# Attention's product with v in plain fp32, two heads side by side in the array, and x written as one tensor

## The chip, the cores and the metric

The kernel runs on one core of a Trainium2 chip. The metric is the device time of one execution in microseconds (us), less is better. Five engines work side by side, each in its own instruction order: PE (TensorE, matrix products and transposes, results in PSUM), DVE (VectorE), ACT (ScalarE), POOL (GpSimd, which reads and writes SBUF alone) and SP (SyncE, which here only issues DMAs). PSUM has eight banks of 128 x 512 fp32.

## The reference

Attention over 4 batches of 8 heads with 576 tokens and 64 columns a head, then two dense layers over all 2304 tokens:

```python
q_rot, k_rot = (rotate(q), rotate(k))
scores = scale * np.matmul(q_rot, k_rot.transpose(0, 1, 3, 2))
scores = scores - np.max(scores, axis=-1, keepdims=True)
attn = np.exp(scores)
attn = attn / (np.sum(attn, axis=-1, keepdims=True) + 1e-09)
x = np.matmul(attn, v)                      # (4, 8, 576, 64), then to (2304, 512)
...
h = np.maximum(x @ w_in, 0.0);  x = h * h @ w_out          # w_in 512 x 2048, w_out 2048 x 512
h = x @ w_in2;  g = np.maximum(h, 0.0) + alpha * np.minimum(h, 0.0);  out = g @ w_out2
```

All of it is fp32 (the weights arrive as 64-bit numbers and are converted on the chip).

## The kernel before

**Products.** Where the kernel wants more than one fp32r pass carries, it splits an operand into a high part (a copy rounded to fp32r) and a low part (the value minus its high part) and adds up fp32r products of the parts. Transposes go through PE with an identity, in fp32.

**Attention.** Two heads of a batch make a pair, 16 pairs in all. A pair has nine steps (`order`): four blocks of 128 queries for each of two heads j, and one step for the last 64 queries of both heads. One loop runs over all 144 steps s. In step s it issues the scores of step s (`scores`, L208: a high and a low product with k into a PSUM tile `sc`; DVE takes the negated row maximum `nm`, L211; ACT takes the exponential into `p` with the row sums, L212) and, four steps later (LAG), the transposes of that step's P (`trans`, L229: four 128 x 128 transposes into a bank `ps`; `trans_tail`, L241 to L248, for the last 64 keys). `split` empties the bank: ACT copies the high part `pth` (L217), then DVE subtracts it from the same bank into the low part `ptl` (L218). Both read PSUM, one after the other, and only then is the bank free. There are three such banks (`ps_t`), shared with the transposes of the next pair's rotated k and q.

**The next pair's k and q.** `turn(n + 1)` runs in steps 0, 1 and 2 of pair n: transposes of k and q (L155, L161) into `ps` banks, a split into `nat` (ACT L149, then DVE L150), and in `stack` (L176) twelve DMAs on SP that lay out `kH`, `kL` and `qT` for the scores of the next pair. Scores of pair n + 1 wait for these DMAs.

**The product with v.** `vsplit` (POOL, L133 and L134) splits v of one pair and lays high and low side by side, so that a head's v has 128 columns: 64 high and 64 low. `pv(n, j, hf, st)` is one head's product for one half of the queries (288): five chunks of 128 keys, for each a product with `pth` and one with `ptl`, ten matmuls of 288 columns into one PSUM bank `acc` (the only one, NAC = 1), rows 0 to 63 from v's high and 64 to 127 from its low part. DVE (L277) or ACT (L279) copies the bank to `st`. A pair has four such bursts, in the steps OP + x * OPD after its last transposes (0, 2, 4 and 6 steps later). `xd` in device memory has two addends per head (the two row halves), written with one DMA per head (L281). `over` (L257 to L265) writes one over the row sums to `rd`.

**The dense layers.** `load_x` reads both addends (L514) and the row factors (L516), `join_x` adds the addends (L524) and multiplies (L525) on POOL, then x is split too (L533, L541). The first two blocks of 384 tokens (FIRST) and the first weights are read and converted in the last 24 steps of attention (AHEAD_X), in `follow`. From there on PE runs the layers' products (L550 to L552, L568) while DVE and ACT convert weights.

**What sets the order.** PE's and SP's order is the order of the code (manual schedule), since the loop above emits it step by step; `at_step` puts a function into a later step. On DVE, ACT and POOL a scheduler orders attention's work by its estimates; in the dense layers their order too is by the code.

Of the kernel before, what the change touches and what calls it, by code (L numbers as in the profile page):

```python
# [22 lines left out]
P = 128  # L23
KC = DM // P
# [10 lines left out]
KQB, STB, PTB = 2, 2, 3  # L35
RB = 1
ROPE_AT, TURN_AT = 5, (0, 1, 2)
AHEAD_X = 24
OP0, OPD0, OP1, OPD1 = 1, 1, 0, 1
OP, OPD, OV = 0, 2, 11  # L40


def attention(tc, q, k, v, ident_d, rope_d, xd, rd, follow):
# [10 lines left out]
    with ExitStack() as at:  # L54
# [12 lines left out]
        lds.append(scored.enter_context(tc.tile_pool(name="ald1", bufs=1)))  # L67
# [21 lines left out]
        raw = {(x, nm): lds[(x, nm) == (1, "v")].tile([P, 4, 5, D], F32, name=f"{nm}raw{x}") for x in range(2) for nm in "kqv"}  # L89
# [36 lines left out]
        vv, ops = {}, {}  # L126

        def vsplit(n):

            x = raw[n // 2 % 2, "v"][:, 2 * (n % 2):2 * (n % 2) + 2]  # L130
            t = sm.tile([P, 2, NQ, 2, D], F32R, name="vs", bufs=KQB)
            hi, lo = t[:, :, :, 0], t[:, :, :, 1]
            G.tensor_copy(out=hi, in_=x)  # L133
            G.tensor_tensor(out=lo, in0=x, in1=hi.bitcast(F32), op=ALU.subtract)  # L134
            vv[n] = t

# [78 lines left out]
        def split(dst, src, sl):  # L215
            hi, lo = dst
            A.activation(out=sl(hi), in_=src, func=AF.Copy)  # L217
            V.tensor_tensor(out=sl(lo), in0=src, in1=sl(hi).bitcast(F32), op=ALU.subtract)  # L218

        def trans(n, i, j):  # L220

            if (i, j) == (0, 0):
                PT[n, "tail"] = tuple(pt.tile([P, S], F32R, name=f"ptt{x}", bufs=2) for x in "hl")
            if i == 0:
                PT[n, j] = tuple(pt.tile([P, 4, S], F32R, name=f"pt{x}") for x in "hl")
# [5 lines left out]
            if i < 4:  # L231
                split(PT[n, j], uv, lambda t: t[:, :, i * P:(i + 1) * P])
            else:
                for x in range(2):
                    split(PT[n, x], uv[:, :, 64 * x:64 * x + 64], lambda t: t[:, :, 512:576])

        def trans_tail(n, i0, i1):
# [5 lines left out]
            if m:  # L243
                split(PT[n, "tail"], u[:, 0:m * P], lambda t: t[:, i0 * P:(i0 + m) * P])
            if i1 == 5:
# [3 lines left out]
                for x in range(2):  # L249
                    rs, u0 = slice(64 * x, 64 * x + 64), (m + x) * P + 64 * x  # L250
                    split(PT[n, "tail"], u[rs, u0:u0 + 64], lambda t: t[rs, 512:576])
# [15 lines left out]
        def pv(n, j, hf, st):  # L267
            vs = vv[n]
            sl = slice(hf * SH, (hf + 1) * SH)
            acc = ps_t.tile([P, 512], F32, name="ps", tag="t") if (n, j) == (len(pairs) - 1, 1) else ps_a.tile([P, 512], F32, name="acc")  # L270
            for c in range(NQ):
                for x in range(2):
                    t = PT[n, j][x][:, c, sl] if c < 4 else PT[n, "tail"][x][:, sl]
                    T.matmul(acc[:, 0:SH], lhsT=vs[:, j, c].rearrange("p y d -> p (y d)"), rhs=t,  # L274
                             start=(c == 0 and x == 0), stop=(c == 4 and x == 1))
            if hf == 0:
                V.tensor_copy(out=st[j][:, sl], in_=acc[:, 0:SH])  # L277
# [32 lines left out]
        at_step(0, vsplit, 0)  # L310
# [3 lines left out]
        for s in range(len(steps) + LAG + OP + 3 * OPD + 8):  # L314
            if s < len(steps):
                n, i, j = steps[s]
                at = s % per
                if at == 0 and n + 1 < len(pairs):
                    at_step(s + OV, vsplit, n + 1)
                    for x, (f, *a) in zip(TURN_AT, turn(n + 1)):  # L320
                        at_step(s + x + (1 if n == 0 else 0), f, *a)
                if at == ROPE_AT and n + 2 < len(pairs):
# [5 lines left out]
                    if n % 2 and n + 3 < len(pairs):  # L328
                        for nm in "kqv":
                            load((n + 3) // 2, nm)  # L330
                scores(n, i, j)
            if LAG <= s and s - LAG < len(steps):
# [3 lines left out]
                if (i, j) == ((2, 1) if last else (3, 1)):  # L336
                    trans_tail(n, 0, 3 if last else 4)
                    sts[n] = [sm.tile([P, S], F32, name=f"st{x}", bufs=STB) for x in range(2)]
                    for x in range(2 if last else 0):
                        at_step(s + OP0 + x * OPD0, pv, n, x, 0, sts[n])  # L340
                if (i, j) == (4, 0):
                    trans_tail(n, 3 if last else 4, 5)
                    at_step(s, over, n)
                    for x in range(4):
                        if not last:
                            at_step(s + OP + x * OPD, pv, n, x % 2, x // 2, sts[n])
                        elif x // 2:
                            at_step(s + OP1 + x % 2 * OPD1, pv, n, x % 2, 1, sts[n])
# [75 lines left out]
def moe(tc, xd, rd, mats, pbias, dram, al, out):  # L424
# [11 lines left out]
    with ExitStack() as mo:  # L436
# [7 lines left out]
        XT = pool("xt", 1, side="right").tile([P, 2, 3, W], F32, name="xt")  # L444
# [63 lines left out]
        def load_x(layer, b, c):  # L508
            c0 = b * W
            k = next(xbuf)  # L510
            xr, r = XT[:, k, 0:2], XT[:, k, 2]
            if layer == 0:
                for j in range(2):
                    nc.sync.dma_start(out=xr[64 * j:64 * j + 64],  # L514
                                      in_=xd[j, :, c, c0:c0 + W].rearrange("(y d) c -> d y c", y=2))
                    nc.sync.dma_start(out=r[64 * j:64 * j + 64], in_=rd[c, j:j + 1, c0:c0 + W].to_broadcast([D, W]))  # L516
            else:
                nc.sync.dma_start(out=xr[:, 0], in_=x2[:, c, c0:c0 + W])
            xin[layer, b, c] = xr, r

        def join_x(layer, b, c):
            xr, r = xin[layer, b, c]
            if layer == 0:
                G.tensor_tensor(out=xr[:, 0], in0=xr[:, 0], in1=xr[:, 1], op=ALU.add)  # L524
                G.tensor_tensor(out=xr[:, 0], in0=xr[:, 0], in1=r, op=ALU.mult)  # L525

        def high_x(layer, b, c):
# [4 lines left out]
            if first(layer, b):  # L532
                G.tensor_copy(out=xh, in_=xin[layer, b, c][0][:, 0])  # L533
# [214 lines left out]
```

## Time and profile before

| | us |
|---|---|
| three runs | 1148.27, 1149.08, 1150.41; median 1149.08 |
| span of the profiled execution, first to last instruction | 1145.5 |
| median less span | 3.6 |
| PE busy in the span | 1082.2 (94%) |
| DVE, ACT, POOL busy | 684.6, 573.1, 374.5 |
| one pair in the middle of attention | 18.29 |
| attention's last product with v starts | about 337 |
| first dense product starts | about 339.5 |

The page gives no time of its own for the profiled execution beyond its span, so its own time is taken as the span with the 3.6 us around it. Attention takes the first 340 us and the dense layers the other 805. A row of the chain of waits (the critical chain) gives a start, a length and the engine and line on which the program's end hung there; a row of waits gives who waited for whom, the sum, the count and the longest; a row of a stretch gives the busy time of each engine in it (instructions in brackets), the granted TensorE clock, the DMA engines' mean busy share and GB/s.

### The profile page before, as it was taken

How to read it: one execution, taken by the hardware profiler on the slowest of the kernel's cores; microseconds unless marked ns; L12 is line 12 of the kernel's file. 1: busy time of each engine (PE TensorE's matmuls, PEld its weight loads, DVE VectorE, ACT ScalarE, POOL GpSimd, SP SyncE). 2: the span in 40 equal slices, each digit the busy share in tenths (PEclk: the TensorE clock that was granted, in tenths of full speed). 3: DMA queues.
4: the chain of work that ended last, by engine and by line, in shares of the span. 5: the costliest groups of instructions: out<-in, count | busy, mean ns of one | idle time of the engine just before them, and what ended most of it. 6: DMA issues, size and time to landing. Idle time of an engine off the chain costs nothing.

```text
span 1145.5 us, 17940 instructions
## 1 busy us (share of the span) xinstructions
PE 1082.2 (94%) x6480; PEld 1031.5 (90%) x6480; DVE 684.6 (60%) x1215; ACT 573.1 (50%) x1236; POOL 374.5 (33%) x360
## 2 busy tenths in 40 slices
PE   2899999999879999999999999999999999999997
PEld 1789898988779999899999999998999989898996
DVE  3888888888678997769597751323232323323231
ACT  1787888878648864465555634223232322323231
POOL 3885558755640000132131311041321405032230
PEclk9999999999989999999999999999999999999999
DMA  6768666775774443557767558810101020010101
GB/s 150 179 181 215 181 167 164 207 199 158 192 214 138 147 129 92 180 184 229 234 207 251 181 180 255 280 51 16 40 8 50 1 50 7 21 35 14 29 1 27
DMA packets 97495, 150.18 MB, mean 131 GB/s; under 512 B 21760, under 2 KB 66432, under 8 KB 97408
## 3 DMA queue, kind: packets, MB, share of 16 engines
q1 hardware_dynamic: 91312, 137.96, 42.3%
q10 hardware_dynamic: 5840, 10.96, 2.9%
q8 instruction: 51, 0.84, 0.3%
q14 instruction: 36, 0.29, 0.1%
q0 software_dynamic: 256, 0.13, 0.0%
HBM read 84.98 MB, written 35.73 MB: 105 GB/s over the span
## 4 chain that ended last, share of the span: by engine, by line
PE 81%; DVE 6%; DMA 5%; SPq 4%; issue 1%; ACT 1%; POOL 1%; ACTq 0%; DVEq 0%; POOLq 0%
PE py L568 31%; PE ph L550 11%; PE ph L552 11%; PE ph L551 11%; PE acc L274 5%; PE sc L208 4%; PE ps L229 3%; SPq L176 3%; PE ph L568 2%; DMA kraw<-in_k_dram 2%; DVE nat L150 2%; DMA xt<-x 1%; DMA xt<-r 1%; DVE ptl L218 1%; DVE nm L211 1%
## 5 line engine op out<-in xcount | busy, mean ns | idle before, releaser
L550 PE MATMUL ph<-xs,w 128*128 128x384 f32 x768 | 256.9, 334 | 1.0 <-ACT g L590 1.0
L551 PE MATMUL ph<-xs,w 128*128 128x384 f32 x768 | 256.7, 334 | 0.0
L552 PE MATMUL ph<-xs,w 128*128 128x384 f32 x768 | 256.6, 334 | 0.0
L503 DVE TENSOR_TENSOR gl<-g,gh 128x384 fp32r<-128x384 f32 x192 | 111.0, 581 | 169.7 <-PE py L568 112.1
L594 POOL TENSOR_TENSOR g<-g,xt 128x384 f32<-128x384 f32 x96 | 101.9, 1062 | 295.5 <-DVE xt L593 295.5
L590 ACT ACTIVATE g<-ph 128x384 f32<-128x384 f32 x192 | 94.3, 491 | 201.6 <-PE ph L552 192.6
L496 ACT ACTIVATE gh<-g 128x384 fp32r<-128x384 f32 x192 | 100.3, 523 | 150.7 <-PE py L568 135.5
L568 PE MATMUL py<-w,gh 128*128 128x512 f32 x504 | 155.3, 389 | 0.0
L568 PE MATMUL py<-gh,w 128*128 128x384 f32 x560 | 145.7, 334 | 0.0
L550 PEld LDWEIGHTS ph<-xs,w 128*128 128x128 f32 x768 | 144.3, 188 | 1.5 <-ACT g L590 1.3
L551 PEld LDWEIGHTS ph<-xs,w 128*128 128x128 f32 x768 | 144.3, 188 | 0.2
L552 PEld LDWEIGHTS ph<-xs,w 128*128 128x128 f32 x768 | 144.3, 188 | 0.0
L593 DVE TENSOR_SCALAR xt<-ph,al 128x384 f32<-128x384 f32 x96 | 59.3, 618 | 138.8 <-ACT g L590 132.2
L212 ACT ACTIVATE p<-sc,nm 128x576 f32<-128x576 f32 x144 | 106.5, 741 | 23.5 <-DVE nm L211 8.6
L211 DVE TENSOR_REDUCE nm<-sc 128x1 f32<-128x576 f32 x144 | 105.7, 750 | 16.7 <-PE sc L208 15.2
L218 DVE TENSOR_TENSOR ptl<-ps,pth 128x512 fp32r<-128x512 f32 (+1 forms) x160 | 99.7, 631 | 20.7 <-ACT pth L217 18.3
L568 PEld LDWEIGHTS py<-w,gh 128*128 128x128 f32 x504 | 94.5, 188 | 19.4
L217 ACT ACTIVATE pth<-ps 128x512 fp32r<-128x512 f32 (+1 forms) x160 | 87.0, 554 | 40.9 <-PE ps L229 35.3
L568 PEld LDWEIGHTS py<-gh,w 128*128 128x128 f32 x560 | 101.5, 188 | 0.0
L568 PE MATMUL py<-w,gl 128*128 128x512 f32 x252 | 98.1, 389 | 0.0
L229 PE MATMUL ps<-ident,p 128*128 128x128 f32 x576 | 87.9, 276 | 8.2 <-DVE nat L150 7.4
L568 PE MATMUL py<-gl,w 128*128 128x384 f32 x280 | 93.6, 334 | 1.9 <-DVE gl L503 1.9
(119 smaller groups left out, 1904.2 us busy)
## 6 DMA issues: line engine op xcount, KB each, us to landing
w<-in_moe_w_in_dram SPq DMA_DIRECT2D x32, 512.0 KB
w<-in_moe_w_out_dram SPq DMA_DIRECT2D x32, 512.0 KB
wk<-xs SPq DMA_DIRECT2D x32, 512.0 KB
w<-wk SPq DMA_DIRECT2D x30, 512.0 KB
xt<-x SPq DMA_DIRECT2D x72, 192.0 KB
x<-st ACTq DMA_DIRECT2D x32, 288.0 KB
kH<-nat SPq DMA_DIRECT2D x62, 144.0 KB
qT<-nat SPq DMA_DIRECT2D x62, 144.0 KB
```

The source lines that it names most:

```text
L211: V.tensor_reduce(out=nm, in_=sc[:, :, 0:SH], axis=AX.XY, op=ALU.max, negate=True)
L212: A.activation(out=Pt[n, i][:, j * S:(j + 1) * S].rearrange("p (a b) -> p a b", a=2), in_=sc[:, :, 0:SH], func=AF.Exp, bias=nm, accum_out= ...
L218: V.tensor_tensor(out=sl(lo), in0=src, in1=sl(hi).bitcast(F32), op=ALU.subtract)
L229: T.transpose(u[:, c * P:(c + 1) * P], p[:, (S + 64) * j + c * P:(S + 64) * j + (c + 1) * P], ident)
L496: A.activation(out=hi, in_=hidden(layer, b, i), func=AF.Copy)
L503: V.tensor_tensor(out=lo, in0=hidden(layer, b, i), in1=gsp[u][0].bitcast(F32), op=ALU.subtract)
L550: T.matmul(ph[:, :W], lhsT=wh[:, cs], rhs=xh, start=(c == 0), stop=False)
L551: T.matmul(ph[:, :W], lhsT=wh[:, cs], rhs=xl, start=False, stop=False)
L552: T.matmul(ph[:, :W], lhsT=wl[:, cs], rhs=xh, start=False, stop=(c == KC - 1))
L568: T.matmul(acc, lhsT=x, rhs=y, start=(s0 and k == 0), stop=(s1 and k == 2))
L590: A.activation(out=g, in_=ph, func=AF.Relu)
L594: G.tensor_tensor(out=g, in0=g, in1=mn, op=ALU.add)
```

## The change

The P transposed leaves PSUM in one copy (`leave`), by ACT and DVE in turn, as fp32. `vsplit` and its pieces are gone: `pv` takes v as it was loaded, in fp32, with 64 columns. Both heads of a pair go into one PSUM bank: head 0 into rows 0 to 63, head 1 into rows 64 to 127, which are the two column halves of the array. A matmul per head and chunk of keys stands alone now (fp32 with fp32), head 0 and head 1 in turn. The work of a pair is cut into six pieces (`LUMPS`: for each half of the queries two chunks, two chunks, one chunk), one piece a step, beginning one step after the pair's last transposes. The last pair runs each half of the queries in one piece. `xd` holds one tensor, written once a pair, and `join_x` only multiplies. v's buffers move to another pool, v's load is issued 16 steps later than k's and q's (V_AT), and P transposed has two buffers of each name instead of three.

```diff
-KQB, STB, PTB = 2, 2, 3
+KQB, STB, PTB = 2, 2, 2
-ROPE_AT, TURN_AT = 5, (0, 1, 2)
+ROPE_AT, TURN_AT, V_AT = 5, (0, 1, 2), 21
+LUMPS = ((0, 0, 2), (0, 2, 4), (0, 4, 5), (1, 0, 2), (1, 2, 4), (1, 4, 5))
-OP, OPD, OV = 0, 2, 11
+OP, OPD = 1, 1
...
-        def split(dst, src, sl):
-            hi, lo = dst
-            A.activation(out=sl(hi), in_=src, func=AF.Copy)
-            V.tensor_tensor(out=sl(lo), in0=src, in1=sl(hi).bitcast(F32), op=ALU.subtract)
+        turns = itertools.cycle((A, V))
+
+        def leave(dst, src):
+            E = next(turns)
+            if E is A:
+                A.activation(out=dst, in_=src, func=AF.Copy)
+            else:
+                V.tensor_copy(out=dst, in_=src)
...
-        def pv(n, j, hf, st):
-            vs = vv[n]
+        accs = {}
+
+        def pv(n, hf, c0, c1):
+            b, hp = pairs[n]
+            v2 = raw[n // 2 % 2, "v"][:, 2 * (n % 2):2 * (n % 2) + 2]
             sl = slice(hf * SH, (hf + 1) * SH)
-            acc = ps_t.tile([P, 512], F32, name="ps", tag="t") if (n, j) == (len(pairs) - 1, 1) else ps_a.tile([P, 512], F32, name="acc")
-            for c in range(NQ):
-                for x in range(2):
-                    t = PT[n, j][x][:, c, sl] if c < 4 else PT[n, "tail"][x][:, sl]
-                    T.matmul(acc[:, 0:SH], lhsT=vs[:, j, c].rearrange("p y d -> p (y d)"), rhs=t,
-                             start=(c == 0 and x == 0), stop=(c == 4 and x == 1))
+            if c0 == 0:
+                accs[hf] = ps_t.tile([P, 512], F32, name="ps", tag="t") if (n, hf) == (len(pairs) - 1, 1) else ps_a.tile([P, 512], F32, name="acc")
+            acc = accs[hf]
+            for c in range(c0, c1):
+                for j in range(2):
+                    t = PT[n, j][:, c, sl] if c < 4 else PT[n, "tail"][:, sl]
+                    T.matmul(acc[64 * j:64 * j + 64, 0:SH], lhsT=v2[:, j, c], rhs=t, start=c == 0, stop=c == 4)
+            if c1 < NQ:
+                return
...
-            A.activation(out=st[j][:, sl], in_=acc[:, 0:SH], func=AF.Copy)
-            b, hp = pairs[n]
-            nc.scalar.dma_start(out=xd[j, :, hp, b * S:(b + 1) * S], in_=st[j])
+            A.activation(out=sts[n][:, sl], in_=acc[:, 0:SH], func=AF.Copy)
+            nc.scalar.dma_start(out=xd[:, hp, b * S:(b + 1) * S], in_=sts.pop(n))
...
             if layer == 0:
-                G.tensor_tensor(out=xr[:, 0], in0=xr[:, 0], in1=xr[:, 1], op=ALU.add)
-                G.tensor_tensor(out=xr[:, 0], in0=xr[:, 0], in1=r, op=ALU.mult)
+                G.tensor_tensor(out=xr, in0=xr, in1=r, op=ALU.mult)
```

PE in the middle of a pair, before: the end of one burst (head 0) and the start of the next (head 1), with two steps of scores (`sc`) and transposes (`ps<-ident,p`) between.

```order
L274 MATMUL acc_1676<-ptl_1420,vs_1341 128x288
L274 MATMUL acc_1676<-ptth_1417,vs_1341 128x288
L274 MATMUL acc_1676<-pttl_1418,vs_1341 128x288
L208 MATMUL sc_1689<-kH_1349,qT1_123 128x288 x2
L208 MATMUL sc_1689<-kL_1350,qT1_123 128x288 x2
L229 MATMUL ps_1701<-ident_77,p_1538 128x128 x4
L208 MATMUL sc_1731<-kH_1349,qT1_123 128x288 x2
L208 MATMUL sc_1731<-kL_1350,qT1_123 128x288 x2
L229 MATMUL ps_1741<-ident_77,p_1538 128x128 x4
L274 MATMUL acc_1748<-pth_1450,vs_1341 128x288
L274 MATMUL acc_1748<-ptl_1451,vs_1341 128x288
```

The same place of PE in the changed kernel: the end of the second piece, the third piece (last chunk, both heads) and the start of the fourth.

```order
L273 MATMUL acc_1486<-pt0_1241,vraw0_111 64x288
L273 MATMUL acc_1486<-pt1_1275,vraw0_111 64x288
L198 MATMUL sc_1531<-kH_1188,qT1_120 128x288 x2
L198 MATMUL sc_1531<-kL_1189,qT1_120 128x288 x2
L223 MATMUL ps_1539<-ident_77,p_1397 128x128 x4
L273 MATMUL acc_1486<-ptt_1240,vraw0_111 64x288 x2
L198 MATMUL sc_1549<-kH_1188,qT1_120 128x288 x2
L198 MATMUL sc_1549<-kL_1189,qT1_120 128x288 x2
L223 MATMUL ps_1557<-ident_77,p_1397 128x128 x4
L273 MATMUL acc_1563<-pt0_1241,vraw0_111 64x288
L273 MATMUL acc_1563<-pt1_1275,vraw0_111 64x288
```

Two heads alternate within a piece, and a piece stands in every step instead of a burst in every second one.

DVE around the next pair's k and q (`nat`), before: steps 0 to 2 of a pair.

```order
L211 TENSOR_REDUCE nm_1868<-sc_1863 128x1
L150 TENSOR_TENSOR nat_1826<-ps_1856,nat_1826 128x512
L218 TENSOR_TENSOR ptl_1700<-ps_1871,pth_1699 128x4x128
L211 TENSOR_REDUCE nm_1891<-sc_1886 128x1
L150 TENSOR_TENSOR nat_1826<-ps_1878,nat_1826 128x512
L218 TENSOR_TENSOR ptl_1740<-ps_1894,pth_1739 128x4x128
L218 TENSOR_TENSOR pttl_1698<-ps_1901,ptth_1697 128x512
L150 TENSOR_TENSOR nat_1826<-ps_1913,nat_1826 128x2x2x64
L211 TENSOR_REDUCE nm_1937<-sc_1932 128x1
```

The same place of DVE in the changed kernel.

```order
L201 TENSOR_REDUCE nm_1600<-sc_1595 128x1
L201 TENSOR_REDUCE nm_1625<-sc_1620 128x1
L140 TENSOR_TENSOR nat_1593<-ps_1613,nat_1593 128x512
L212 COPY pt0_1479<-ps_1628 128x4x128
L201 TENSOR_REDUCE nm_1647<-sc_1642 128x1
L140 TENSOR_TENSOR nat_1593<-ps_1634,nat_1593 128x512
L212 COPY ptt_1478<-ps_1656 128x512
L201 TENSOR_REDUCE nm_1686<-sc_1681 128x1
L140 TENSOR_TENSOR nat_1593<-ps_1662,nat_1593 128x2x2x64
```

Between the three `nat` rows two copies stand where three subtractions stood, and one row of `nm` comes earlier.

SP's queue at the very start, before: the last loads of k and q for the first pairs, and the first DMAs of `stack`.

```order
L99 DMA qraw_113<-in_q_dram 128x2x256
L107 DMA qraw_113<-in_q_dram 64x2x64 x2
L712 DMA al<-in_moe_alpha_dram 128x16x1
L176 DMA kH<-nat 64x576
L176 DMA qT_122<-nat 64x576
```

The same place in the changed kernel.

```order
L99 DMA qraw_110<-in_q_dram 128x2x256
L107 DMA qraw_110<-in_q_dram 64x2x64 x2
L386 DMA w_4004<-in_moe_w_in_dram 128x4x256
L386 DMA w_4006<-in_moe_w_in_dram 128x4x256
L708 DMA al<-in_moe_alpha_dram 128x16x1
L166 DMA kH<-nat 64x576
L166 DMA qT_119<-nat 64x576
```

Two loads of first-layer weights (512 KB each), which before stood among the loads of the last attention steps, stand at the program's start, ahead of the first pair's `stack`: their buffers no longer lie where attention's tiles lie.

## Rows read from the trace of the kernel before

**Rows 1.** The page: span, and busy time of each engine.

```profile
span 1145.5 us, 17940 instructions
PE 1082.2 (94%) x6480; PEld 1031.5 (90%) x6480; DVE 684.6 (60%) x1215; ACT 573.1 (50%) x1236; POOL 374.5 (33%) x360
```

**Rows 2.** Stretches: busy us of each engine, granted clock, DMA share, GB/s.

```profile
60.00:90.00 30.00, 27.51 (x219) 26.27 (x218) 26.82 (x50) 24.27 (x62) 23.63 (x20) 1.00 0.66 176
...
330.00:360.00 30.00, 24.94 (x133) 24.39 (x134) 21.89 (x44) 16.52 (x35) 4.30 (x4) 0.89 0.45 137
360.00:390.00 30.00, 30.00 (x175) 30.00 (x175) 27.74 (x52) 25.30 (x48) 0.00 (x0) 1.00 0.52 157
```

**Rows 3.** The chain of waits through one pair: start us, us, engine and line.

```profile
159.03 0.11 PE ps L247
159.14 0.11 PE ps L248
159.25 0.14 PE ps L260
159.39 1.32 PE acc L274 x10
...
161.23 0.44 PE ps L229 x4
...
168.87 0.53 PE sc L208 x4
...
177.68 0.40 PE acc L274 x3
```

**Rows 4.** Waits of PE from 42 to 282 us: sum us, times, longest us.

```profile
PE ps L161 <- DVE nat L150: 9.1, 13, 0.7
PE ps L229 <- DVE nat L150: 6.9, 13, 0.6
```

**Rows 5.** Groups by line, 60 to 280 us: busy us, mean ns of one.

```profile
L274 PE MATMUL acc<-ptl,vs 128*128 128x288 f32 x194 | 52.8, 294 | 0.0
...
L218 DVE TENSOR_TENSOR ptl<-ps,pth 128x512 fp32r<-128x512 f32 (+1 forms) x121 | 75.4, 631 | 11.4 <-ACT pth L217 9.5
...
L150 DVE TENSOR_TENSOR nat<-ps,nat 128x512 fp32r<-128x512 f32 (+1 forms) x36 | 21.5, 598 | 3.1 <-ACT nat L149 2.7 <-DMA kraw<-in_k_dram 0.3
...
L217 ACT ACTIVATE pth<-ps 128x512 fp32r<-128x512 f32 (+1 forms) x120 | 65.2, 555 | 24.2 <-PE ps L229 24.2
```

**Rows 6.** SP's queue after one turn: start us, us of the issue.

```profile
176.91 1.15 SPq L176 DMA_DIRECT2D kH<-nat  x2
...
183.41 1.23 SPq L176 DMA_DIRECT2D kL<-nat  x2
```

**Rows 7.** The chain early in attention: a `kL` DMA from issue to landing.

```profile
40.53 2.98 DMA kL<-nat
```

**Rows 8.** The start: SP's queue, and a stretch of four us.

```profile
7.50 0.59 SPq L712 DMA_DIRECT2D al<-in_moe_alpha_dram  x1
...
12.00:16.00 4.00, 1.54 (x6) 1.14 (x6) 2.17 (x6) 0.96 (x3) 1.65 (x2) 1.00 0.00 0
```

**Rows 9.** Waits of PE from 282 to 365 us.

```profile
PE ps L247 <- DVE pttl L218: 3.2, 1, 3.2
PE sc L208 <- DMA kL<-nat: 2.7, 2, 1.7
PE ps L260 <- DVE sums L258: 2.1, 1, 2.1
...
PE ps L260 <- DVE pttl L218: 0.9, 1, 0.9
PE ps L229 <- DVE ptl L218: 0.8, 1, 0.8
```

**Rows 10.** PE's instructions at the end of attention: start us, us, engine line.

```profile
337.06 0.44 PE L274 MATMUL ps<-pth,vs 128*128 128x288 f32 x1
337.31 0.44 PE L274 MATMUL ps<-ptl,vs 128*128 128x288 f32 x1
...
339.46 0.52 PE L550 MATMUL ph<-xs,w 128*128 128x384 f32 x1
```

More of the change, by code (lines that the diff above doesn't have):

```diff
@@ L86, in attention @@
         rot = {}
-        raw = {(x, nm): lds[(x, nm) == (1, "v")].tile([P, 4, 5, D], F32, name=f"{nm}raw{x}") for x in range(2) for nm in "kqv"}
+        raw = {(x, nm): (st_ if nm == "v" else lds[0]).tile([P, 4, 5, D], F32, name=f"{nm}raw{x}") for x in range(2) for nm in "kqv"}
         for x in range(2):
@@ L124, in rope @@
             E.tensor_tensor(out=r, in0=t1, in1=t2, op=ALU.add)
[L126 to L135, printed above, removed]
+        ops = {}
         qTs = [kq.tile([P, 2 * S + 64], F32R, name=f"qT{x}", bufs=1) for x in range(2)]
@@ L243, in trans_tail @@
             if m:
-                split(PT[n, "tail"], u[:, 0:m * P], lambda t: t[:, i0 * P:(i0 + m) * P])
+                leave(PT[n, "tail"][:, i0 * P:(i0 + m) * P], u[:, 0:m * P])
             if i1 == 5:
@@ L250, in trans_tail @@
                     rs, u0 = slice(64 * x, 64 * x + 64), (m + x) * P + 64 * x
-                    split(PT[n, "tail"], u[rs, u0:u0 + 64], lambda t: t[rs, 512:576])
+                    leave(PT[n, "tail"][rs, 512:576], u[rs, u0:u0 + 64])
         def over(n):
@@ L308, in at_step @@
             later.setdefault(s, []).append((f, a))
-        at_step(0, vsplit, 0)
         rope(1, "k")
         rope(1, "q", E=V)
-        for s in range(len(steps) + LAG + OP + 3 * OPD + 8):
+        for s in range(len(steps) + LAG + OP + len(LUMPS) * OPD + 8):
             if s < len(steps):
@@ L328, in attention @@
                     if n % 2 and n + 3 < len(pairs):
-                        for nm in "kqv":
+                        for nm in "kq":
                             load((n + 3) // 2, nm)
+                        at_step(s - ROPE_AT + V_AT, load, (n + 3) // 2, "v")
                 scores(n, i, j)
@@ L337, in attention @@
                     trans_tail(n, 0, 3 if last else 4)
-                    sts[n] = [sm.tile([P, S], F32, name=f"st{x}", bufs=STB) for x in range(2)]
-                    for x in range(2 if last else 0):
-                        at_step(s + OP0 + x * OPD0, pv, n, x, 0, sts[n])
+                    if last:
+                        at_step(s + OP0, pv, n, 0, 0, 5)
                 if (i, j) == (4, 0):
@@ L442, in moe @@
         Xw = [Xf[:, 1024 * k:1024 * k + 1024].rearrange("p (y n) -> p y n", y=2) for k in range(6)]
-        XT = pool("xt", 1, side="right").tile([P, 2, 3, W], F32, name="xt")
+        XT = pool("xt", 1, side="right").tile([P, 2, 2, W], F32, name="xt")
         st = [pool("st0", 1, side="right")]
@@ L701, in fused_kernel @@
     nc.gpsimd.memset(pbias, -float(896 * 2 ** 23))
-    xd = dram.tile([2, P, KC, NT], F32, name="x1")
+    xd = dram.tile([P, KC, NT], F32, name="x1")
     rd = dram.tile([KC, 2, NT], F32, name="r1")
```

36 lines of the change are left out of this document (17 added, 19 removed).

## The prediction

> **What bounds the kernel now.** I read the page first, for who is busy at all. PE is busy for 1082.2 of 1145.5 us [rows 1], so only PE's own work and the few places where it waits can pay. Then the stretches. In the dense layers PE is busy for 30.00 of 30 us [rows 2], and the change touches nothing there but how x is read and joined; I count nothing after 360 us. In attention PE has 27.51 of 30 us, DVE 26.82 and ACT 24.27 [rows 2]: PE leads, and DVE is so close behind that PE must wait for it somewhere. The chain of waits through one pair says where the time goes: from 159.39 to 177.68 is one pair, 18.29 us, nearly all of it PE's own work [rows 3]. The waits of PE name the rest: 9.1 + 6.9 = 16.0 us over 13 pairs, 1.23 us a pair, all of it PE's transposes waiting for a PSUM bank that DVE empties last, in the turn of the next pair's k and q [rows 4]. So attention is PE's work plus 1.23 us a pair that DVE owes. At the end of attention PE waits more: 3.2, 0.9 and 0.8 us for DVE's splits and 2.1 us for the row sums that stand behind them [rows 9], and after that idling its last ten products come 0.25 us apart instead of 0.132 [rows 10, 3], in a stretch whose granted clock is 0.89 [rows 2].
>
> **DVE and ACT: less work.** A pair has 13 splits, a high copy on ACT and a subtraction on DVE each. In 220 us they take 75.4 us of DVE and 65.2 of ACT (without the small tail pieces) [rows 5]. Now each bank is emptied once, by one of the two in turn. I price a copy like the subtraction it replaces (631 ns in the mean [rows 5]; it reads the same bank), so half of each remains: DVE gives back about 37 of 220 us, 3.1 us a pair, and ACT about as much. That by itself is off the path; what pays are the banks that come free earlier. Before, a bank is held for an ACT copy and a DVE subtraction in series, 555 + 631 ns without queues [rows 5]; now for one of them. The split of `nat` (598 ns on DVE behind its copy on ACT [rows 5]) stays as it was, and the order of DVE still has an `nm` ahead of each `nat`, so I take 80% of the 16.0 us: **-12.8 us**. Ends: 0 (the `nat` split alone holds the bank) and -16.0.
>
> **PE: the product with v.** Taken away are 4 bursts of 10 fp32r matmuls a pair, 1.32 us each, 0.132 us a matmul [rows 3], 5.28 us a pair. Added are 20 fp32 matmuls of the same 288 columns but half the width. No row shows an fp32 product; the nearest rows bound it. From below: an fp32 transpose moves 128 columns in 0.11 us (four in 0.44 [rows 3]); at that price per column 288 take 0.248 us. From above: the kernel's own way to a full product is four fp32r products of parts (high and low of P with high and low of v), so one fp32 matmul costs 4 x 0.132 = 0.528 us. I take the upper price, because the partial products that make up the result are the same four, and a transpose multiplies by ones and needs fewer.
>
> The two heads use different column halves. Whether both run at once is the question of this change, and no row answers it. If they do, a pair's product costs 10 x 0.528 = 5.28 us, exactly what it cost: the same partial products on the same area of the array. If they don't, 20 x 0.528 = 10.56. I take the first: nothing that the two halves need is shared but the issue, and issue is not what bounds a matmul here (0.132 us for 288 columns against 0.11 for 128 [rows 3], so it is columns that cost). **0 us** for the product, ends -45 (10 x 0.248 = 2.48, 16 pairs x 2.80) and +84 (16 x 5.28).
>
> The Trainium skill ("TensorE: Matmul & The Clock Gate", Part 3, measured speedup) lets column tiles run concurrently and measured 2.38 times for three of them. Scaled to two halves that is an estimate of 1.59, which would make the product 6.65 us a pair and the forecast below about 1157; no run here shows it yet.
>
> **PE: twelve switches of tile width a pair.** Each of six pieces goes from 128 columns to halves and back. The trace of before has such switches: the 64-column transpose (L247) and the 32-column one (L260) stand between full-width ones, and the chain gives 0.11, 0.11 and 0.14 us for L247, L248 and L260 where a full-width transpose takes 0.11 [rows 3]. Four switches cost 0.03 us together at most; I take 0.015 each, 12 x 16 x 0.015 = **+2.9 us**, with 0 as the other end.
>
> The Trainium skill ("TensorEngine Tiling (Array Packing)", Key Properties) says that a change of tiling mode drains the engine, which speaks against this change. The rows just named show no drain of that size, so here the trace and the rule part, at least for transposes; what the rule would make of the time is a rival below.
>
> **The end of attention.** Of the 4.9 us of waits for splits I count half, since one of two serial steps goes, of the 2.1 us behind the sums half for the same reason, and the 1.1 us that the last ten products lose (337.06 to 339.46, 2.40 us instead of 1.32) [rows 9, 10, 3]: 2.5 + 1.0 + 1.1 = **-4.6 us**. Ends 0 (the first dense product then waits for x or weights instead) and -8.1. x's own path gets shorter (one addend to load, one POOL pass less), and two of the first weights' loads move to the start, so I expect nothing there to be late first.
>
> **Edits at nothing.** The two weight loads at the start are issued at about 7.5 us, ahead of the first `stack`, and have a stretch with a DMA share of 0.00 from 12 to 16 us to run in [rows 8]; without that cover their two issues would cost about 1.2 us. `vsplit` leaves POOL, which is busy for a third of the span [rows 1]. The later load of v and its wait stand in SP's queue behind that turn's `stack` DMAs, which nobody else waits behind. Half the x stores and x loads: DMAs with other work above them. The one bank `acc` must be copied out by DVE between the third and the fourth piece; scores and transposes of 0.97 us lie between, and DVE has room now.
>
> **What is late next.** The `stack` DMAs: the last is issued by 184.64 and lands 2.98 us later [rows 6, 7], 187.6, while the scores of the next pair start at 168.87 + 18.29 = 187.2 [rows 3] and need its second half a step, about 1 us, later. The slack is about half a microsecond. But the two waits that go lie ahead of `nat`, so the DMAs move forward with them, and I charge nothing.
>
> **Sum.** 1149.1 (span 1145.5 plus the 3.6 around it) - 12.8 + 0 + 2.9 - 4.6 = 1134.6, so **1135 us**. Its own range by the ends of waits, switches and tail is 1125 to 1147.
>
> **Rivals.**
> *Staggered halves (slower).* If one fp32 matmul is run as two half-matmuls in series and PE starts matmuls strictly in order, head 1 of a chunk begins only with the second half of head 0. In a long run that costs nothing, but each piece then begins and ends with 0.264 us in which one half of the array is idle: 0.264 x 6 x 16 = +25 us, 1160. It decides from 14.5 / 96 = 0.15 us of lone time a piece. For it: the chain shows PE's matmuls strictly one after the other [rows 3]. Against: an fp32 transpose shows no second pass of its own there.
> *Quarter overlap.* With four serial passes the overlap is only one in four; a piece of two chunks takes 13 passes and one of one chunk 7, 66 x 0.132 = 8.7 us a pair, +55: 1190.
> *No overlap.* +84: 1219.
> *Drain at each switch.* If it exposes the tail of a matmul, the 294 ns of one [rows 5] less the 132 between two, 0.162 us, then 192 x 0.162 = 31 instead of 2.9 us: 1163. That is the time by the page's rule on tiling modes; the rows give it little.
> *Cheap fp32.* At the price of a transpose: 1135 - 45 = 1090.
> *The change does not relieve PE.* The waits stay or pass to the `stack` DMAs, 1147.
>
> **Chances.** Forecast 0.43, staggered 0.18, drain 0.06, quarter 0.06, no overlap 0.11, cheap fp32 0.06, no relief 0.06, the rest 0.04 on either side. The range leaves out no overlap and cheap fp32 and reaches from the best end of the forecast to the quarter case: 1124 to 1190. A difference of 0.2% (2.3 us) is about what a measurement can tell. Faster: 0.43 + 0.06, a fifth of the staggered case (lone times under 0.13 us) and half of the rest, 0.55. Within 0.2%: 0.08. Slower: 0.37. Forecast alone: 1125 to 1147.
>
> **What would show it.** In the changed kernel's chain a piece of four products should take about 1.06 us and one of two 0.53; 1.32 and 0.79 mean a stagger, 2.1 no overlap. Full-width work right behind a piece should start with no gap; 0.16 us would be the drain. The waits of PE for `nat` should be under 4 us in all, a pair about 17.5 us (18.29 - 0.98 + 0.18), DVE near 22 us of 30 in attention, and the first dense product should start about 15 us earlier, near 325. The forecast is wrong if the two halves run one after the other, or if PE's waits move to `qT` and `kL` DMAs.

## The result, and the profile after

The changed kernel takes **1163.09 us** (median of 4 runs, 1160.55 to 1166.08) where the kernel before, beside it, takes 1148.92: 1.0124 times as long, 95% interval 1.0104 to 1.0145. It is slower by 14 us; 1135 us had been forecast, and the range (1124 to 1190) holds the time. The profiled execution took 1164.05 us, 1.8 more than its span of 1162.3; so the one before, with its span of 1145.5, took about 1147.3 and not the 1149.1 that was taken for it. The spans are therefore 16.8 us apart where the medians are 14.

The page of the changed kernel, span and busy time of each engine:

```profile
span 1162.3 us, 17534 instructions
PE 1108.2 (95%) x6480; PEld 987.0 (85%) x6480; DVE 615.5 (53%) x1094; ACT 526.2 (45%) x1116; POOL 311.3 (27%) x304
```

Against [rows 1], DVE gave back 69 us, ACT 47 and POOL 63, as the change promised. PE, the engine that bounds the kernel, has as many records as before (half the products with v, two records for each) and is busy for 26 us more.

Stretches of the changed kernel, columns as in [rows 2]:

```profile
60.00:90.00 30.00, 28.83 (x211) 21.52 (x209) 19.06 (x33) 18.21 (x46) 19.02 (x16) 1.00 0.48 122
...
360.00:390.00 30.00, 26.53 (x144) 26.21 (x143) 26.07 (x49) 23.89 (x45) 0.00 (x0) 0.94 0.41 127
```

DVE fell from 26.82 to 19.06 of 30 us and is nowhere near PE any more. PE rose from 27.51 to 28.83 with fewer records in the same 30 us (211 for 219): a record costs more. New is the last row: PE has 26.53 where it had all 30.00, at a granted clock of 0.94.

Where the 16.8 us lie is read from one instruction that comes once a pair, the transpose of the row sums. First before (its first, 14th and last), then after, with the first dense product (the one of before is in [rows 10]); start us, us, engine, line:

```profile
49.17 0.29 PE L260 MATMUL ps<-ident,sums 128*32 128x128 f32 x1
287.19 0.28 PE L260 MATMUL ps<-ident,sums 128*32 128x128 f32 x1
334.47 0.40 PE L260 MATMUL ps<-ident,sums 128*32 128x128 f32 x1 [2.08 <-DVE sums L258]
```

```profile
51.34 0.27 PE L254 MATMUL ps<-ident,sums 128*32 128x128 f32 x1 [0.55 <-DVE nat L140]
308.35 0.27 PE L254 MATMUL ps<-ident,sums 128*32 128x128 f32 x1 [0.62 <-DVE nat L140]
347.45 0.28 PE L254 MATMUL ps<-ident,sums 128*32 128x128 f32 x1 [0.80 <-DVE sums L252]
351.86 0.44 PE L546 MATMUL ph<-xs,w 128*128 128x384 f32 x1
```

| stage | before, us | after, us | difference |
|---|---|---|---|
| start to the first transpose of sums | 49.17 | 51.34 | +2.2 |
| 13 pairs | 238.02 (18.31 each) | 257.01 (19.77 each) | +19.0 |
| the last two pairs | 47.28 | 39.10 | -8.2 |
| to the first dense product | 4.99 | 4.41 | -0.6 |
| dense layers to the end of the span | 806.04 | 810.44 | +4.4 |

So a regular pair got 1.46 us longer where the forecast had it 0.8 us shorter, the end of attention gained more than forecast, and the dense layers, where nothing had been expected, gave half of that back.

The chain through one pair of the changed kernel (start us, us, engine, line; `acc L273` is the product with v, x8 a piece of four products, x4 one of two, since each fp32 product leaves two records; `sc L198` scores, `ps L223` and `ps L145` transposes):

```profile
150.22 0.27 PE ps L254
150.49 0.53 PE sc L198 x4
151.01 0.44 PE ps L223 x4
151.45 1.12 PE acc L273 x8
152.57 0.72 PE sc L198 x4
153.29 0.44 PE ps L223 x4
...
156.01 0.64 PE acc L273 x4
156.65 0.73 PE sc L198 x4
...
163.69 0.59 PE ps L145 x4
...
165.25 0.44 PE ps L145 x4
...
170.00 0.27 PE ps L254
```

This is the reading that matters. One chunk more (two products, one for each head) costs 1.12 - 0.64 = 0.48 us, so two chunks are 0.97 of the 1.12: 0.15 us of a piece is no product. And what stands behind a piece is longer than elsewhere: four scores 0.72 instead of 0.53, four transposes of k 0.59 instead of 0.44. In and out together a piece pays about **0.34 us** beside its work, six times a pair: 2.05 us. The work itself is 10 x 0.485 = 4.85 us, 0.43 less than the 5.28 of before. 2.05 - 0.43 = +1.62 of the measured +1.46.

The waits of PE in the changed kernel from 42 to 282 us (us in total, times, longest), which answer to [rows 4]:

```profile
PE ps L254 <- DVE nat L140: 7.3, 12, 0.6
...
PE ps L151 <- ACT pt L210: 0.8, 5, 0.2
PE ps L151 <- DVE pt L212: 0.7, 2, 0.6
```

The two waits of [rows 4], 16.0 us, are all but gone from the tail transposes of the turn (L161 before, L151 now) and from those of P. 7.3 us stand in a new place: the transpose of the sums waits for the bank of the last `nat`. The waits by name are 9.0 us now, but PE's whole stretch from the turn's first transpose of q to the transpose of the sums hardly got shorter: 4.99 us before, 4.83 and 4.92 in turn now. The rest stands in gaps that no row names. DVE's rows at the end of the turn say why the transpose of the sums waits (start us, us, engine, line; in brackets the idle time before):

```profile
167.62 0.68 DVE L140 TENSOR_TENSOR nat<-ps,nat 128x512 fp32r<-128x512 f32 x1
168.77 0.76 DVE L201 TENSOR_REDUCE nm<-sc 128x1 f32<-128x576 f32 x1 [0.46 <-PE sc L198]
169.44 0.41 DVE L140 TENSOR_TENSOR nat<-ps,nat 128x256 fp32r<-128x256 f32 x1
```

DVE sat idle for 0.46 us, waiting for scores, with the `nat` that PE needs next standing behind that `nm` in its queue; before, the last `nat` stood ahead of that `nm`. A faster DVE doesn't help such a wait: the order of its queue makes it. In the next pair DVE works from 184.69 us to the last `nat` without a pause, but there too an `nm` (188.52) stands ahead of it (189.19).

At the end, the waits of PE from 282 to 365 us, which answer to [rows 9], and ACT's last copy of x with the conversion behind it:

```profile
PE ph L546 <- ACT g L586: 3.5, 1, 3.5
PE ps L241 <- ACT ptt L210: 2.0, 1, 2.0
...
PE ps L254 <- DVE sums L252: 0.8, 1, 0.8
```

```profile
351.98 0.41 ACT L280 ACTIVATE st<-ps 128x288 f32<-128x288 f32 x1 [3.94 <-PE ps L273]
...
352.81 0.76 ACT L405 ACTIVATE w<-w,pbias 128x512 uint32<-128x512 uint32 x1 [0.42 <-ACT st L280]
```

The waits of attention's end fell from the 9.7 us in the rows of [rows 9], 13.0 with the smaller ones, to 4.9. But ACT now stands for 3.94 us in front of the copy of the last half of x, and the conversions of the next weights stand behind it, and `g` behind those: PE waits 3.5 us for `g` where it had waited 1.0.

### The profile page after: what moved, and what is told of

The parts are those of the page before. It is cut to its first block, busy times and chain, and to the rows that moved or that the text cites. A ratio compares the mean times of both kernels' runs of the same rounds, so it can differ in the third digit from the quotient of the medians.

```text
span 1162.3 us, 17534 instructions
## 1 busy us (share of the span) xinstructions
PE 1108.2 (95%) x6480; PEld 987.0 (85%) x6480; DVE 615.5 (53%) x1094; ACT 526.2 (45%) x1116; POOL 311.3 (27%) x304
## 4 chain that ended last, share of the span: by engine, by line
PE 83%; DVE 6%; SPq 4%; DMA 3%; issue 1%; ACT 1%; ACTq 0%; DVEq 0%
PE py L564 31%; PE ph L546 11%; PE ph L548 11%; PE ph L547 11%; PE acc L273 6%; PE sc L198 6%; PE ps L223 3%; PE ph L564 2%; DVE nm L201 2%; SPq L166 2%; DVE nat L140 1%; DMA qraw<-in_q_dram 1%; DVE pt L212 1%; SPq L107 1%; SPq L103 1%
## 5 line engine op out<-in xcount | busy, mean ns | idle before, releaser
L201 DVE TENSOR_REDUCE nm<-sc 128x1 f32<-128x576 f32 x144 | 108.7, 755 | 104.8 <-PE sc L198 103.7
L198 PE MATMUL sc<-kH,qT 128*128 128x288 f32 x336 | 83.7, 335 | 10.0 <-DMA qT<-nat 7.6
L223 PE MATMUL ps<-ident,p 128*128 128x128 f32 x576 | 88.0, 276 | 2.6 <-ACT pt L210 0.7
L198 PEld LDWEIGHTS sc<-kH,qT 128*128 128x128 f32 x336 | 51.4, 193 | 45.1 <-issue 29.2
```

The lines of the kernel that those rows point to most:

```text
L198: T.matmul(sc[:, hf, o0:o0 + w], lhsT=lhs, rhs=kx[:, c0:c0 + w], start=st and y == 0, stop=not st and y == len(prods) - 1 and o0 + w == SH)
L201: V.tensor_reduce(out=nm, in_=sc[:, :, 0:SH], axis=AX.XY, op=ALU.max, negate=True)
L223: T.transpose(u[:, c * P:(c + 1) * P], p[:, (S + 64) * j + c * P:(S + 64) * j + (c + 1) * P], ident)
```

## Experiments

The kernel before was run beside each group of experiments, and its median lay between 1147.97 and 1150.36 us. A difference of a few us between two versions is therefore taken from their ratios to it.

### Fewer pieces: is it the pieces that cost?

```diff
-LUMPS = ((0, 0, 2), (0, 2, 4), (0, 4, 5), (1, 0, 2), (1, 2, 4), (1, 4, 5))
-OP, OPD = 1, 1
+LUMPS = ((0, 0, 5), (1, 0, 5))
+OP, OPD = 1, 3
```

> The changed kernel with a pair's product with v in two pieces of five chunks (one a half of the queries, three steps apart) instead of six. Theory (each change between full-width and half-width work costs PE 0.15 us going in and 0.19 us coming out, 0.34 us a piece): four pieces a pair fewer, 4 x 0.34 x 15 pairs = -20 us, about 1143, and a piece takes 20 rounds-of-two, ten of 0.243 us, plus 0.15. Rival (the edge is not a switch but the halves starting one after the other): also fewer edges, -4 x 0.26 x 15 = -16, but then single half-products stand alone at a piece's ends. Rival (the edges are hidden elsewhere, DVE and ACT set the pair): no change, 1163.

Measured: 1154.11 us (6 runs), 1.0056 of before (1.0033 to 1.0080). That is 8 us less than the changed kernel by the ratios (9.0 by the times alone), not the 20 that 15 pairs of four pieces fewer would give. Every second pair does have the gain: 18.46 us instead of 19.77, 1.31 less where four prices of 0.34 make 1.36. The others take 19.25 to 19.56. Here is the chain, and behind it the waits from 42 to 282 us:

```profile
165.92 2.58 PE acc L273 x20
168.50 0.73 PE sc L198 x4
```

```profile
PE sc L198 <- ACT p L202: 4.5, 12, 0.4
PE ps L254 <- DVE nat L140: 3.8, 7, 0.6
PE ps L151 <- DVE pt L212: 3.8, 6, 0.7
```

Five chunks take 2.58 = 5 x 0.485 + 0.15, and the scores behind them 0.73 again: the price is a piece's, not a product's. But with the products in two lumps, several steps of scores follow each other with nothing between, and PE waits for ACT's exponentials (4.5 us; the changed kernel has one such wait, of 1.3) and for `pt` (3.8 for 0.7). These waits explain a part of the rest; the whole of it is not accounted for.

### The same products at full width: is it the width?

```diff
-T.matmul(acc[64 * j:64 * j + 64, 0:SH], lhsT=v2[:, j, c], rhs=t, start=c == 0, stop=c == 4)
+w = v2[:, j, min(c, 3):min(c, 3) + 2].rearrange("p c d -> p (c d)")
+T.matmul(acc[:, 0:SH], lhsT=w, rhs=t, start=c == 0 and j == 0, stop=c == 4 and j == 1)
```

> The changed kernel with every product with v at the full 128 columns (fp32 still, two neighbouring chunks of v as weights, both heads into the same rows), so its sums mix heads and chunks: a price, not the reference's result. Theory (the edge comes from the change of width): a piece of four products takes 8 x 0.243 = 1.94 us with no edge, the scores behind it their plain 0.53 us, a pair 19.78 - 2.0 + 4.86 = 22.6 us, about 1208. Rival (the edge comes from the change between fp32 and fp32r products): edges stay, a pair 24.6 us, about 1240.

Measured: 1207.61 us (one run), as the theory had it. Its chain:

```profile
162.45 1.94 PE acc L274 x8
164.40 0.52 PE sc L198 x4
...
168.26 0.97 PE acc L274 x4
```

Four fp32 products of 128 columns in width take 1.94 us, two take 0.97: strictly in proportion, and the scores behind them take their plain 0.53. Both extra times, 0.15 in and 0.19 out, are gone with the same data type, the same pieces and the same places. What a piece pays for is the change of the array's width. Lone narrow transposes still pay nothing: in the changed kernel the 64-column one and the full one behind it start at 169.00 and 169.11 us, 0.11 apart as ever. Why these go without the price no run here says.

### Both heads in one half: do the halves run side by side?

```diff
+first = ((0, 0), (0, 1)) if last else ((0, 0), (2, 0))
-T.matmul(acc[64 * j:64 * j + 64, 0:SH], ..., start=c == 0, stop=c == 4)
+x = j if (c == 4 or last) else c // 2
+T.matmul(acc[64 * x:64 * x + 64, 0:SH], ..., start=(c, j) in first, stop=c == 4)
```

> The changed kernel with a piece's four products all in one half of the array (chunks 0 and 1 of both heads in the first half, 2 and 3 in the second; the fifth chunk stays as it was), so that the two heads can't run side by side; the number of products and of pieces stays, the sums mix heads and chunks. If the two heads were side by side in the changed kernel: a piece's records follow one another, 8 times 0.243 us instead of 4 times, four such pieces a pair, 15 pairs: +58, 1221. If it is the two records of one fp32 product that start together, whichever half they are in: no change, 1163.

Measured: 1213.68 us (one run), 50.6 above the changed kernel; 58 had been worked out, and of the rest 4.3 us are waits at L254 that the longer pieces cover (3.0 us for 7.3). Its chain:

```profile
166.61 2.08 PE acc L276 x8
168.69 0.73 PE sc L198 x4
```

2.08 is 8 x 0.243 + 0.14, where the changed kernel has 4 x 0.243 + 0.15. So in the changed kernel the two heads did run side by side, fully: without the entry the ratio is 2.0. And the entry and the 0.73 behind stay, with one half in use at a time, the first or the second: they belong to the width, not to two halves starting together.

### The heads in a row

```diff
-for c in range(c0, c1):
-    for j in range(2):
+for j in range(2):
+    for c in range(c0, c1):
```

> The changed kernel with the products of a piece in another order: all chunks of head 0, then all of head 1, instead of head 0 and head 1 in turn. Theory (two records that start 6 ns apart are the two heads, in the two column halves): nearly no overlap is left, a piece of four products takes some 7 to 8 rounds of 0.243 us instead of 4, a pair 3 to 5 us more, 1210 to 1240. Rival (the two records are the two passes of one product, side by side, and the heads run one after the other anyway): no change, 1163.

Measured: 1168.21 us (one run). In its chain a piece is the same as in the changed kernel:

```profile
152.81 1.13 PE acc L273 x8
```

The expectation fell. With the products of one head in a row the two halves still run side by side: the records start in pairs again, 14 ns apart (6 in the changed kernel), and the run before this one shows that two records of one half follow one another. So PE starts the first product of the other half ahead of one that waits for its own half. But it doesn't reach far. The last pair has ten products in a piece, five of a head in a row; the chain, first of the changed kernel, then of this run:

```profile
340.55 2.58 PE acc L273 x20
```

```profile
342.15 4.08 PE acc L273 x20
```

PE's records in the second of these pieces (`ptt` is the last chunk, `pt` the four others):

```profile
342.08 2.21 PE L273 MATMUL acc<-pt,vraw 128*64 128x288 f32 x10
344.07 0.41 PE L273 MATMUL acc<-ptt,vraw 128*64 128x288 f32 x1
```

Ten records of `pt` start ahead of the first of `ptt`, where head 0 has only eight in front of it: the first product of head 1 did overtake. But it starts at 343.59 us, 1.51 after head 0's first, when only one product of head 0 is left waiting ahead of it. With two products of a head in a row the order costs nothing, with five it costs 1.50 us. A regular pair is 19.8 us as in the changed kernel. Of the 5 us more in this single run 1.5 are this piece, and 1.3 lie ahead of the first transpose of sums (52.6 us); the runs of the changed kernel spread over 5.5 us.

### The relief alone

The kernel before, with each bank of transposes emptied by one copy:

```diff
-A.activation(out=sl(dst[0]), in_=src, func=AF.Copy)
-V.tensor_tensor(out=sl(dst[1]), in0=src, in1=..., op=ALU.subtract)
+E = next(turns)     # ACT, DVE in turn
+... one copy to sl(dst[0])
-PT[n, j] = (high, low)
+PT[n, j] = (high, high)
```

> This is the kernel before with every bank of transposes emptied once, by one engine in turn, so that ACT and DVE have the work of the changed kernel while TensorE keeps its 40 products with v and its width of 128 columns (the low part of P transposed is left out: the low product reads the high tile). It measures the relief by itself. The prediction's own sum: 1149 - 12.8 (waits in the pairs) - 4.6 (end of attention) = 1132. What the changed kernel's trace says instead: the waits in the pairs only change their place (a transpose of the sums behind a nat that now stands behind an nm), and about 12 us go at the end of attention alone: 1137. If there is no relief anywhere: 1148 to 1149.

Measured: 1139.73 us (2 runs), 0.991 of before (0.9886 to 0.9934): well below no relief, and above both other figures, nearer to 1137. Three transposes of the sums in a row:

```profile
210.76 0.28 PE L264 MATMUL ps<-ident,sums 128*32 128x128 f32 x1
228.89 0.27 PE L264 MATMUL ps<-ident,sums 128*32 128x128 f32 x1 [0.62 <-DVE nat L150]
246.28 0.28 PE L264 MATMUL ps<-ident,sums 128*32 128x128 f32 x1
```

The 13 regular pairs take some 18.13 and 17.39 us in turn (17.76 in the mean), and this is worth more than the sum. In one kind DVE's order has an `nm` ahead of the last `nat`, in the other `nat` comes first (a pair has an odd number of copies, so the engines' turns swap from pair to pair). Where `nat` comes first a pair gains 0.92 us on the 18.31 of before, near the 0.98 that the forecast took for the waits; where it doesn't, 0.18. In the changed kernel it comes second in every pair. The end of attention, from the 14th transpose of the sums (281.78 us) to the first dense product (329.94), takes 4.1 us less than before, near the 4.6 of the forecast and far from the 12 that had been read from the changed kernel.

### The transpose of the sums one step later

```diff
-at_step(s, over, n)
+at_step(s + 1, over, n)
```

> The changed kernel with one edit: the transpose of the sums (over) is issued one step later, behind the next four scores and the transposes, so that the bank it needs has been emptied when TensorE comes to it. Theory (the wait of 0.62 us at L254 is what took the place of the waits before): the twelve waits of 7.3 us between 42 and 282 us and those of the two pairs behind go, 1163 - 8.5 = 1154.5. Rival (DVE's late nat holds back the next bank as well): the wait moves to the transposes of the next step, 1161 to 1164.

Measured: 1157.8 us (4 runs), 1.0064 of before (1.0046 to 1.0083): by the ratios 6.9 us less than the changed kernel (5.3 by the times alone), of 8.5. The waits from 42 to 282 us:

```profile
PE ps L223 <- DVE nat L140: 1.8, 4, 0.6
```

The wait is off the sums, and about a quarter of it turns up here, at the next transposes that need the bank. A pair takes 19.2 and 19.5 to 20.2 us in turn, 19.47 in the mean: the relief in the pairs is then 0.46 us (18.31 + 1.62 - 19.47), near the 0.55 of the run above, instead of 0.16.

### Both, and the last copy later

With two pieces as well:

> Two pieces a pair instead of six, as in e1_two_pieces (1154), and the transpose of the sums one step later, as in e6. If the two gains add: 1154 less the 3.8 to 4.5 us that e1 waited at L254 = 1150, the same as the kernel before. If the waits of the scores on ACT's exponentials (0.44 us a pair in e1, where eight steps follow one another without a product between them) take up the gain: 1153 to 1155. Below 1146 only if PE's order also loses the wait at L151 (3.8 us in e1).

Measured: 1150.55 us (10 runs), 1.0009 of before (0.9998 to 1.0021). The gains add; the waits for ACT's exponentials and at L151 stay as they were with two pieces.

At the start of the dense layers, the changed kernel with ACT's copy of the last half of x two steps later, behind the first conversion:

```diff
-A.activation(out=sts[n][:, sl], in_=acc[:, 0:SH], func=AF.Copy)    # last pair, second half
+at_step(s + OP1 + PUT, lambda n: put(n, accs[1]), n)               # PUT = 2; put: the same copy and store
```

> The changed kernel with one edit at the end of attention: ACT copies the last half of the output of the last pair two steps later, behind the first conversion of the next weight tile, instead of ahead of it. Theory (the 4.4 us that the dense part lost are ACT's: the conversion w waits behind a copy that waits for the last product, and g, in row behind the conversions, lets TensorE wait 3.5 us and start again at half clock): the wait of 3.5 us goes to under 1 and with it the half clock, 1163 - 4 to 5 = 1158 to 1159. Rival (the conversions are bound by their own chain of ACT and DVE): 1162 to 1164.

Measured: 1157.41 us (4 runs), 1.0083 of before (1.0066 to 1.0099), by the ratios 4.7 us less than the changed kernel (5.7 by the times alone), as expected. ACT's rows:

```profile
348.96 0.76 ACT L412 ACTIVATE w<-w,pbias 128x512 uint32<-128x512 uint32 x1 [1.29 <-DMA r<-ri]
...
352.42 0.41 ACT L286 ACTIVATE st<-ps 128x288 f32<-128x288 f32 x1 [1.24 <-PE ps L274]
```

The conversion starts at 348.96 instead of 352.81, and no wait for `g` is left among PE's waits. The first dense product starts at 352.30 us of a span of 1155.9, so the dense layers take 803.6 us, 6.8 less than in the changed kernel. So the 4.4 us of the dense layers were ACT's, by the order of its queue.

> Two pieces a pair, the transpose of the sums one step later, and the late last copy: e7 (1150.5) and e10 together. If the gains add: 1145.5 to 1146.5, faster than the kernel before by 0.2 to 0.4%. If the late copy brings nothing: 1150, the same as before.

Measured: 1148.09 us (11 runs), 0.9999 of before (0.9990 to 1.0008). By the ratios the late copy brings 1.1 us here, within the noise, not 4 to 5: PE still waits 1.5 us for `g`. With two pieces and both orders mended the kernel is as fast as before, to 0.1%.

### The same product in bf16

P transposed and v are rounded to bf16 (v by POOL), so a product has one pass in place of fp32's two; all else as in the changed kernel.

```diff
-PT[n, j] = pt.tile([P, 4, S], F32, name=f"pt{j}")
+PT[n, j] = pt.tile([P, 4, S], BF16, name=f"pt{j}")
-lhsT=v2[:, j, c]
+lhsT=vb[n][:, j, c]
```

> The changed kernel with P transposed and v in bf16 (v cast by POOL once a pair), still in column halves, so the product is less exact. Theory (width): one record a product, two products a round of about 0.13 us, ten rounds 1.3 us a pair instead of 4.86, and the edges of 0.15 and 0.19 us stay at each of six pieces; a pair about 16.2 us if PE still leads. Rival (fp32 mode): edges vanish, a pair about 14.2 us if PE still leads.

Measured: 1117.6 us (one run). Its chain:

```profile
166.17 0.37 PE acc L278 x4
166.54 0.72 PE sc L203 x4
```

A piece of two chunks takes 0.37 us where one of one chunk takes 0.24, so 0.26 of it are work, and the scores behind it take 0.72 again: 0.11 in and 0.19 out, 0.3 us beside 0.26 of work. A pair without waits is down to 15.37 us; every second one is 17 us or more, because the copies of k and q come late (11.7 us of waits on `kL` and `qT` from 42 to 282 us).

> P transposed and v rounded to bf16, as in e3_bf16_halves (1117.6), with two pieces a pair instead of six and the transpose of the sums one step later. A bf16 piece still pays for the switches of width (about 0.2 us a piece by the trace of e3: the product's second round takes 0.22 us to the scores behind it where 0.12 is the work, and the scores' second record comes 0.24 us after the first instead of 0.13). If four switches in and out fewer a pair come through: 15 x 4 x 0.2 = 12 us, 1106. If e3 is held by the copies of k and q by DMA by now (11.7 us of waits on kL and qT between 42 and 282 us): 1113 to 1118.

Measured: 1121.84 us (4 runs), 0.9765 of before (0.9744 to 0.9786); not below the single run of the six pieces at all. Its waits from 42 to 282 us:

```profile
PE sc L203 <- DMA kL<-nat: 10.5, 15, 2.2
PE sc L203 <- DMA qT<-nat: 10.2, 5, 2.2
PE sc L203 <- ACT p L207: 6.7, 14, 2.6
```

The lumps leave the scores bare, and they run into the copies (20.7 us) and into ACT.

> e3_bf16_halves (P transposed and v rounded to bf16, six pieces a pair, one look: 1117.6) with the late last copy of e10_late_last_copy. If the gain at the start of the dense part is the same as there (TensorE waited 3.0 us for g in e3): 1117.6 - 4 = 1113.5, 0.97 of the kernel before. If one look of e3 was a lucky one, or the copies of k and q hold it: 1117 to 1121.

Measured: **1114.74 us** (4 runs, 1112.63 to 1117.44), 0.9692 of before (0.9662 to 0.9722). The number is near the expectation, but not by its reason: PE still waits 2.1 us for `g`, and the dense layers take 809.8 us where the run without the late copy has 808.9. In these two traces it is the 13 pairs that are shorter, 212.3 us for 216.5, with nothing in the edit that would make them so. The late copy's own gain isn't shown here. This is the fastest version, at the price of P and v in bf16.

## Why the prediction was wrong, step by step

- **Switches of width, +2.9: the step that failed.** It was sized at 0.015 us a switch from transposes of 64 and 32 columns [rows 3] and measured about 0.17, 0.34 for a pair in and out. 90 pieces make +31 us of it. The rows were read rightly, but they were the wrong neighbours: a narrow transpose that stands alone among wide ones showed no such price, and shows none now. The rival *drain at each switch* had 0.162 us, 31 us and 1163, and a price of that size is what came, with a chance of 0.06. The rule of the Trainium skill ("TensorEngine Tiling (Array Packing)", Key Properties), that a change of tiling mode drains the engine, fits these runs: 0.34 us a piece with halves, none in the full-width run. That the time is a drain, and not something else that comes with the width, is not shown. A page's rule that names just what the change does deserved more than two narrow transposes against it. That the rival's sum meets the measured time to the microsecond is luck: it kept the relief of -12.8 and had nothing for the start and the dense layers (+2.2 and +4.4), and the cheaper product and the end of attention, both better than forecast, made up for most of that.
- **Product with v, 0: the mechanism right, the size near.** The halves overlap fully (2.08 against 1.12 us a piece); *staggered*, *quarter* and *no overlap* are out. An fp32 product takes 0.485 us, not 0.528, and not the 0.25 of *cheap fp32*: -0.43 us a pair. The estimate of 1.59, scaled to two tiles from the 2.38 for three of the Trainium skill ("TensorE: Matmul & The Clock Gate", Part 3), isn't borne out; the two halves give 2.0 without the entry, 1.86 with it.
- **Relief of the waits, -12.8: the second step that failed.** What is left of 19.77 - 18.31 = +1.46 after +2.05 and -0.43 is -0.16 us a pair, some -2.5 in all. The working named the reason and took it too lightly: "the order of DVE still has an `nm` ahead of each `nat`". The wait moved to the next transpose that needs the bank. With `nat` ahead the relief is 0.92 a pair, with `nm` ahead 0.18.
- **The end of attention, -4.6.** It gained 8.8 us (-8.2 and -0.6), beyond the end of -8.1. In part that is luck: 4.0 us of waits for `kL`, `qT` and ACT's `p` that the forecast hadn't counted are gone too, and such waits come and go (4.6 us for `qT` and `kL` in the run of the relief alone). "I count nothing after 360 us" failed: +4.4, ACT's copy ahead of the conversions, 3.5 us of idling for `g`, then eleven products of 384 columns 0.32 us apart instead of 0.17, at a granted clock of 0.50 (1.2 GHz) from 364.8 to 368.0 us.
- **The start, 0.** +2.2 us here. Among the runs with the same prologue the first transpose of sums starts between 49.3 and 52.6 us, and with the prologue of before it starts at 49.2 and, in the run of the relief alone, at 50.9. Whether any of the 2.2 us is the change's stays open.
- **What is late next** was right only for the bf16 version: there it is the `stack` copies.
- **The forecast's own range, 1125 to 1147,** isn't the sum of its ends. 1125 takes the best ends of waits, switches and tail together; their worst ends together give 1149.1 + 2.9 = 1152, and 1147 puts only the waits at nothing.

By stage the sum closes: 2.2 + 19.0 - 8.2 - 0.6 + 4.4 = 16.8. That the direction came out wrong hangs on the first step. Without its 31 us the sum is about 1132. No run shows that kernel; the relief alone, at full width and without the price, took 1139.73 us, and the cheaper product would make it about 1133 (15 pairs at 0.43 us less). Of the 20 us that fewer pieces save only 8 to 9 came through, so 1132 is the lowest time to hope for.

## What to carry to other kernels

A run of narrow products side by side in the array has a fixed price, however long it is: count the changes of width, and price one in and out at what a trace shows (0.34 us here) before any gain. When a wait is to go because an engine gets lighter, read that engine's order: if the instruction that frees the buffer stands behind one that waits for something else, the wait stays and only changes its name. And small pieces between other work hide waits that lumps lay bare, so fewer, larger pieces brought less than half of what they save on the changes of width.

## What the runs showed of the hardware

- An fp32 matmul of 288 moving columns leaves two records and takes 2 x 0.243 us, at 128 and at 64 columns of width alike; a bf16 one takes 0.13, an fp32r one 0.132.
- A change of the array's width between 128 and 64 columns around a run of matmuls costs about 0.15 us going in and 0.19 coming out (0.11 and 0.19 in bf16), whether one half or both are used. Lone transposes of 64 and 32 columns between full-width work show no such price (0.11 and 0.14 us [rows 3]).
- Two halves run at once even if the program has the products of one half first, but PE's reach is short: with two products of a head in a row a piece takes the same 1.13 us, with five in a row 4.08 us instead of 2.58, and the other half starts when one product is left waiting ahead of it.
